# Two attentions on one core: the polynomial that VectorE uses for B's exps goes from degree three to degree two

## The chip, the cores and the metric

The kernel runs on one core of a Trainium2 chip. The metric is device time in microseconds (us), the median of three runs. The core has TensorE (PE, matrix products into PSUM), ScalarE (ACT, activations such as exp), VectorE (DVE, elementwise work and reductions), GpSimd (POOL) and SyncE (SP); the last two here mostly issue transfers (DMA).

## The reference

Two attention layers over the same input x (2048 tokens, 512 wide, 32 heads of 16) are mixed by a gate. A has one key and one value head for all query heads; B has its own K and V for every head.

```
q, k, v = ...                                  # x @ wq, x @ wk, x @ wv; A: one k and v, B: one per head
scores = einsum("bhqd,bhkd->bhqk", q, k) * 16 ** -0.5
p = softmax(scores)                            # no mask: 2048 x 2048 for each of 32 heads
o = einsum("bhqk,bhkd->bhqd", p, v)  -> 2048 x 512 @ wo
g = sigmoid((x * gate_w).sum(-1))
out = g * A + (1 - g) * B
```

All tensors are float32. A's wq and wk are eight times larger than drawn, so A's scores span a wide range and B's are small. Both attentions together take 2 x 32 x 2048 x 2048 exps, that is 2048 tiles of 128x1024.

## The kernel before, in words

A fast path is always run. At its end one flag says whether the inputs were inside the limits it assumes; if not, a general path (`_general`) computes everything again behind it. The flag is made from `stats`, a table of maxima (`absmax`, L222) that are taken along the way, reduced and compared in `flag_reduce` and `flag_check` (L1267 to L1285). For B the limit is `B_MAX`: the largest |q| times the largest |k| times the scale, where |q| is the sum of magnitudes over the 16 dimensions of a head (`magnitudes`, L511: a bit mask on VectorE, a small matmul against a matrix of heads, a maximum in PSUM) and |k| is the largest element.

The fast path walks through eight groups in turn, A and B alternating (`groups`, L202), each of eight heads. A group has four *phases* (a half of the queries, a half of the heads), a phase has 32 *quads*, and a quad two tiles of 128x1024 scores. For each tile TensorE writes the transposed scores into a PSUM slot (`products`, L751, matmuls at L762; inputs are split into high and low float16 parts that share the contraction). Then the exp is made in one of two ways:

- ScalarE reads the slot and writes exp to a tile in SBUF (`exp`, L781, the ACTIVATE at L793).
- VectorE makes it as a chain of operations (`chain`, L1000). For A it converts to an integer (L1016), splits off mantissa and power (L1020, L1024) and evaluates a polynomial of degree four (L1029, four times). For B, whose scores are small, a cubic is enough: `first` (L1049) reads PSUM, `second` (L1052) and `third` (L1056) work in SBUF. `first` occupies the PSUM slot, the others do not.

From the exps TensorE accumulates values and row sums in one PSUM slot (`values`, L834, matmuls at L847, float32): V has columns of ones beside it (vB), so sums of exps come out beside sums of exp times V. After 32 quads the phase is emptied into SBUF (L917), the row sums go through DRAM into another layout (`each`), are inverted and multiplied by the gate (`gated`, L673), come back spread over partitions, and the outputs are multiplied by them (`times`, L687) and split for the product with wo (`o_unit`, L575, matmuls at L215). Projections of Q, K and V (`project`, L464, L215) run as *units* of 24 steps in between; those for B's next group fall mostly while A is at work. V is turned by TensorE and copied into vB (L551).

There are four PSUM slots: one collects values, one is lent to a unit or to a VectorE chain (`hold`, L398), and the others pass scores to ScalarE. There are 16 tiles in SBUF for exps.

The order of everything is planned when the program is written, by a small model of the engines (`_Plan`). Each step of TensorE (`pe_step`, L1131) first looks for a score for ScalarE, then for a unit or a chain for VectorE (`spare_job`, L1086), or for values. A chain starts (`vector_job`, L974) when the pending operations of rank 3, the later operations of earlier chains, sum to no more than `WORK`, and enough tiles are free; `pick` (L945) takes the last open quad of the present phase, or, when what is left of the phase is shorter than `CHAIN` and the backlog, the last of the next phase. `hurry` (L1077) says that some unit's due time is near; then units go ahead of chains. `BEGIN` is how many tiles must be free before a long unit starts. VectorE's own queue is in the planned order too (`vector`, L110), by rank and due time; the engine carries it out strictly in that order. SP issues most transfers, in order; V's own copies are spaced.

The end of the kernel (L1532 to L1570) is written out by hand: the last products with wo for the second half of the queries, eight tiles of 128 queries, whose results are added to what earlier groups left (`late`, loaded from `out`), six of them by VectorE (`give`, L1543) and two by ScalarE and an adding transfer (`added`, L1548).

## Time and profile before

| | us |
|---|---|
| median of 3 runs | 1730.31 (1729.32 to 1733.89) |
| profiled execution, its own time | 1731.76 |
| its span, first to last instruction | 1729.9 |
| TensorE busy | 1687.4 (98%), 51451 matmuls |
| weight loads busy | 1008.2 (58%) |
| VectorE busy | 1487.2 (86%), 1658 instructions |
| ScalarE busy | 1665.2 (96%), 1813 instructions |
| GpSimd busy | 195.5 (11%) |
| TensorE clock granted, mean | 0.994 |

Times are of one execution taken by the hardware profiler. A group of instructions is shown as line, engine, operation, output and input names with their shapes, and a count, then the busy time in us, the mean length of one in ns, and the idle time before them with what ended it. Matmuls overlap and their ends are modelled, so a busy TensorE is not one at its peak. The names `prob`, `vec`, `early` and `vB` in the place of exps are all tiles for exps; `slot` is PSUM.

### The profile page before, as it was taken

The numbers are of one execution on the slowest core, as the hardware profiler recorded it, in microseconds if no ns is written. First come the engines' busy times: TensorE is split into PE (matmuls) and PEld (weight loads), VectorE is DVE, ScalarE is ACT, GpSimd is POOL, SyncE is SP. The second block draws the span as 40 slices with busy tenths as digits, with TensorE's granted clock in tenths as the row PEclk, the third lists the DMA queues.
The fourth block names the chain that finished last, engine by engine and source line by source line (L and its number), as shares of the span: only waits on it lengthen the run. The fifth ranks groups of instructions, "written<-read, shape, count | busy, mean of one in ns | idle before, by whom it ended". The sixth has DMA issues, their size and how long they took to land.

```text
span 1729.9 us, 110256 instructions
## 1 busy us (share of the span) xinstructions
PE 1687.4 (98%) x51451; PEld 1008.2 (58%) x51451; DVE 1487.2 (86%) x1658; ACT 1665.2 (96%) x1813; POOL 195.5 (11%) x316
## 2 busy tenths in 40 slices
PE   8999999999999999999999999999999999999996
PEld 5556546456566656666566555665665655655553
DVE  5567699999998899988999888999899898988954
ACT  4999999999999999999999999999999999999994
POOL 1111101000101200011111010111102111111000
PEclk9999999999999999999999999999999999999998
DMA  5212201111212211231222122222213212222312
...
DMA packets 71446, 95.72 MB, mean 55 GB/s; under 512 B 27612, under 2 KB 36092, under 8 KB 70980
## 3 DMA queue, kind: packets, MB, share of 16 engines
...
## 4 chain that ended last, share of the span: by engine, by line
PE 61%; ACT 18%; issue 12%; DVE 7%; DMA 1%; POOL 0%; SPq 0%; ACTq 0%; DVEq 0%; POOLq 0%
PE slot L847 32%; PE slot L762 17%; ACT prob L793 11%; PE slot L215 11%; ACT vec L793 6%; DVE prob L1049 1%; DVE prob L1056 1%; DVE prob L1052 1%; DVE vec L1029 1%; DVE vec L1049 1%; DVE vec L1052 1%; DMA Qa<-hiqa 0%; PE slot L1407 0%; PE slot L309 0%; DVE vec L1016 0%
## 5 line engine op out<-in xcount | busy, mean ns | idle before, releaser
L793 ACT ACTIVATE prob<-slot 128x1024 f32<-128x1024 f32 x1129 | 1121.4, 1101 | 19.3 <-PE slot L762 14.7
L793 ACT ACTIVATE vec<-slot 128x1024 f32<-128x1024 f32 x657 | 685.6, 1099 | 7.6 <-PE slot L762 3.6
L847 PE MATMUL slot<-prob,vB 64*32 64x256 f32 (+3 forms) x8096 | 529.6, 439 | 0.1
L847 PE MATMUL slot<-prob,vA 64*32 64x512 f32 (+3 forms) x7536 | 499.1, 447 | 0.0
L762 PE MATMUL slot<-Qa,kA 64*32 64x512 f16 x8192 | 441.6, 378 | 8.4 <-DMA Qa<-hiqa 2.0
L762 PE MATMUL slot<-Qb,K 64*32 64x512 f16 x8192 | 421.2, 378 | 12.7 <-ACT prob L793 4.6
L847 PE MATMUL slot<-vec,vB 64*32 64x512 f32 (+3 forms) x4640 | 367.8, 434 | 0.8 <-issue 0.7
L847 PE MATMUL slot<-vec,vA 64*32 64x512 f32 (+3 forms) x4656 | 365.7, 446 | 0.0
L762 PEld LDWEIGHTS <-K 64*32 64x32 f16 x8192 | 192.4, 90 | 239.9 <-issue 191.3
L762 PEld LDWEIGHTS <-kA 64*32 64x32 f16 x8192 | 191.8, 90 | 235.4 <-issue 180.8
L847 PEld LDWEIGHTS slot<-prob,vB 64*32 64x32 f32 x8096 | 214.9, 106 | 38.8 <-issue 8.5
L847 PEld LDWEIGHTS slot<-prob,vA 64*32 64x32 f32 x7536 | 199.8, 106 | 43.4 <-issue 14.0
L847 PEld LDWEIGHTS slot<-vec,vB 64*32 64x32 f32 x4640 | 144.7, 106 | 26.6 <-issue 8.3
L847 PEld LDWEIGHTS slot<-vec,vA 64*32 64x32 f32 x4656 | 140.2, 106 | 26.4 <-issue 8.3
L1049 DVE TENSOR_SCALAR prob<-slot 128x1024 f32<-128x1024 f32 x109 | 133.0, 1220 | 17.9 <-PE slot L762 15.1
L1029 DVE SCALAR_TENSOR_TENSOR prob<-prob,prob 128x1024 f32<-128x1024 f32 x83 | 101.1, 1220 | 1.0
L1049 DVE TENSOR_SCALAR vec<-slot 128x1024 f32<-128x1024 f32 x71 | 86.6, 1220 | 12.4 <-PE slot L762 8.2
L215 PEld LDWEIGHTS <-o 64*32 64x32 f16 x3072 | 56.5, 93 | 32.8 <-ACT o L694 6.8
L1016 DVE TENSOR_SCALAR prob<-slot 128x1024 int32<-128x1024 f32 x46 | 56.2, 1221 | 19.4 <-PE slot L762 17.0
L1052 DVE SCALAR_TENSOR_TENSOR prob<-prob 128x1024 f32<-128x1024 f32 x59 | 71.5, 1219 | 0.5
L1056 DVE SCALAR_TENSOR_TENSOR prob<-prob,prob 128x1024 f32<-128x1024 f32 x59 | 71.5, 1218 | 0.2
L1029 DVE SCALAR_TENSOR_TENSOR prob<-prob,vec 128x1024 f32<-128x1024 f32 x55 | 67.0, 1220 | 0.7
(190 smaller groups left out, 1748.5 us busy)
## 6 DMA issues: line engine op xcount, KB each, us to landing
...
```

Source lines behind the costliest of these rows:

```text
L215: nc.tensor.matmul(outs[n : n + COLS, i], lhs[i][rows(i), n : n + COLS], rhs[i][rows(i)], start=start, stop=stop)
L762: nc.tensor.matmul(bank[a : a + COLS, hh], k[rows(hh), key : key + COLS], Q[src, gi, half, p][rows(hh), j * BLK : (j + 1) * BLK], start=Tr ...
L793: nc.scalar.activation(probs[u], sc, AF.Exp, scale=SCALE / (UP * UP))
L847: nc.tensor.matmul(pair[0][32 * k : 32 * k + 32, i, cols], v[rows(i)], probs[2 * m + k // 2][rows(i), hh, cols], start=first, stop=last)
L1016: nc.vector.tensor_scalar(tile("p").bitcast(I32), pair[1], SCALE / (UP * UP) / math.log(2) * 2.0 ** 23, None, op0=ALU.mult)
L1029: nc.vector.scalar_tensor_tensor(p, m if i == 3 else p, VEC[i], m if i else w, op0=ALU.add, op1=ALU.mult)
L1049: nc.vector.tensor_scalar(tile("p"), pair[1], CUBE[0] * SCALE / (UP * UP), CUBE[1], op0=ALU.mult, op1=ALU.add)
L1052: nc.vector.scalar_tensor_tensor(tile("w"), tiles["p"], CUBE[2], tiles["p"], op0=ALU.add, op1=ALU.mult)
L1056: nc.vector.scalar_tensor_tensor(p, w, CUBE[3], p, op0=ALU.add, op1=ALU.mult)
```

## The change

For B's exps on VectorE, with s the scaled score, the cubic is replaced by c0 + c1 s + c2 s s. The chain makes only the last two terms, with the square root of c2 folded in: `first` scales (PSUM to SBUF), `second` is (t + c1 / sqrt(c2)) t, in the same tile. c0 is left out of the tile. It belongs to every key that VectorE made, so its part of the output is c0 times the sum of V over those keys, and its part of the row sum is c0 times their number. `sums_of` takes sums of V over blocks of 64 keys when V is projected (a reduction from PSUM, a scaling, two small copies between the halves of the partitions); `missing` adds up the blocks that a phase's VectorE quads cover; `gated` adds the count to `each`, and `times` adds the sum of V before it multiplies. The very last phase keeps a third operation that adds c0.

The degree-two polynomial is used within |s| of 0.044. The bound becomes length of q times length of k, per head: `norms` replaces `magnitudes` for q and the plain maximum for k (a clamp, a square, the matmul, a maximum), `flag_reduce`, `flag_pairs` and `flag_check` multiply the two for each head.

A chain of B now needs one tile, not two. Several constants of the plan change with it (`BEGIN`, `CHAIN`, `WORK`, the limit in `hurry`, due times), and the hand-written end gives all eight sums to VectorE.

The diff; a line of "..." marks what is left out.

```
@@ -34,24 +34,25 @@
-B_MAX = 0.16
+B_MAX = 0.044
...
-CUBE = (0.5500864384102879, 0.8808852829622843, -0.986763876, 1.22848465)
+SQUARE = (1.0000001191795511, 1.0002430729569356, 0.4999387172344313)
...
+SQUARED, HI_MAX = 16.0, 60000.0
...
-LEFT, LEFT_END, BEGIN = 1, 1, 5
+LEFT, LEFT_END, BEGIN = 1, 1, 4
...
@@ -491,8 +492,8 @@
             def then(end):
...
-                if kind == "q_b":
-                    plan.vec(lambda: magnitudes(2 * gi + half, hilo[0]), 330, 2, end, due=end + 4000, room=spare_tiles)
+                if src == "b" and part != "v":
+                    plan.vec(lambda: norms(kind, 2 * gi + half, hilo[0]), 1400, 2, end, due=end + 4000, room=spare_tiles)
...
@@ -501,20 +502,61 @@
+            def blocks():
+                sums_of(gi, half)
...
+            if part == "v":
+                one = plan.vec(blocks, 1250, 0, 0.0, (one,))
...
-    def magnitudes(n, hi):
+    v_sums = {}
+    def sums_of(gi, half):
+        if half == 0:
+            v_sums[gi] = ops.tile([P, 2, 2 * NT], F32, tag="sums", name=f"sums{gi}", bufs=2)
+        at = slice(NT * half, NT * (half + 1))
+        own, other = v_sums[gi][:, 0, at], v_sums[gi][:, 1, at]
+        nc.vector.tensor_reduce(own, pair[1].rearrange("p e (n k) -> p (e n) k", k=ROWS), axis=AX.X, op=ALU.add)
+        nc.vector.tensor_scalar(own, own, SQUARE[0] * UP ** -2, None, op0=ALU.mult)
+        swapped(other, own, nc.sync)
+        plan.sp += 2 * ISSUE_SP
+    def missing(ph, to):
+        n, half, q = phases[ph]
+        sums = v_sums[n // 2]
+        taken = [divmod(m - 32 * ph, 2) for m in range(32 * ph, 32 * ph + 32) if m in vector]
+        for i in range(2):
+            runs = []
+            for k in sorted(2 * c + (w ^ i) for c, w in taken):
+                if runs and runs[-1][1] == k:
+                    runs[-1][1] += 1
+                else:
+                    runs.append([k, k + 1])
+            for r, (a, b) in enumerate(runs):
+                nc.vector.tensor_reduce(to[rows(i), r : r + 1], sums[rows(i), i ^ (q // 2), a:b], axis=AX.X, op=ALU.add)
+            for r in range(1, len(runs)):
+                nc.vector.tensor_tensor(to[rows(i), :1], to[rows(i), :1], to[rows(i), r : r + 1], op=ALU.add)
+        return len(taken)
+    measured = [0]
+    def norms(kind, n, hi):
...
-        nc.vector.tensor_scalar(mag.bitcast(I32), hi.rearrange("p e t -> p (e t)").bitcast(I32), 0x7FFF7FFF, None, op0=ALU.bitwise_and)
...
+        nc.vector.tensor_scalar(mag, hi, -HI_MAX, HI_MAX, op0=ALU.max, op1=ALU.min)
+        nc.vector.scalar_tensor_tensor(mag, mag, SQUARED / (UP * UP), mag, op0=ALU.mult, op1=ALU.mult)
...
         def job():
...
@@ -524,15 +566,16 @@
         def finish(t):
             def top():
-                nc.vector.tensor_reduce(stats[: 2 * COLS, KINDS.index("q_b"), n : n + 1], pair[1][: 2 * COLS], axis=AX.XY, op=ALU.max)
+                nc.vector.tensor_reduce(stats[: 2 * COLS, KINDS.index(kind), n : n + 1], pair[1][: 2 * COLS], axis=AX.XY, op=ALU.max)
...
             def then(end):
+                measured[0] += 1
...
-        start = plan.dve + 330 + FROM_VEC
-        units.append(_Unit([(job, PRODUCT)], finish, lambda now: now >= start, lambda: start + 12000, f"m{n}"))
+        start = plan.dve + 1400 + FROM_VEC
+        units.append(_Unit([(job, PRODUCT)], finish, lambda now: now >= start, lambda: start + 12000, f"m{kind}{n}"))
...
     def turned(gi, half, hilo, now):
...
@@ -596,9 +639,9 @@
             def take():
...
-                    if last or t == 0:
+                    if last:
...
-                            (nc.sync, nc.scalar if last else nc.sync)[e].dma_start(out[tt[e] * P : (tt[e] + 1) * P, :], mine[:, e])
+                            (nc.sync, nc.scalar)[e].dma_start(out[tt[e] * P : (tt[e] + 1) * P, :], mine[:, e])
...
@@ -626,7 +669,7 @@
-        due = 32 * (LASTS + half) if ends else 32 * (8 * j + 2 * half + 11)
+        due = 32 * (LASTS + half) if ends else 32 * (8 * j + 2 * half + 9)
...
@@ -670,7 +713,15 @@
         def over(c):
...
+        ph = phases.index((n, half, q))
+        short = src == "b" and not ends and any(m in vector for m in range(32 * ph, 32 * ph + 32))
+        if short:
+            lost = ops.tile([P, 16], F32, tag="lost", name=f"lost{n}{half}{q}", bufs=2)
         def gated():
+            if short:
+                count = missing(ph, lost)
+                nc.vector.tensor_scalar(each, each, SQUARE[0] * ROWS * count, None, op0=ALU.add)
...
@@ -688,7 +739,10 @@
-                nc.vector.tensor_tensor(o[:, c : c + cut], o[:, c : c + cut], d[:, c : c + cut], op=ALU.mult)
+                if short:
+                    nc.vector.scalar_tensor_tensor(o[:, c : c + cut], o[:, c : c + cut], lost[:, :1], d[:, c : c + cut], op0=ALU.add, op1=ALU.mult)
+                else:
+                    nc.vector.tensor_tensor(o[:, c : c + cut], o[:, c : c + cut], d[:, c : c + cut], op=ALU.mult)
...
         def high(c):
...
@@ -713,7 +767,7 @@
-        plan.vec(gated, 430, 3.5, now + 7500, (), spreads, min(due, now + 25000),
+        plan.vec(gated, 900 if short else 430, 3.5, now + 7500, (), spreads, min(due, now + 35000),
...
@@ -978,7 +1032,7 @@
-        if u is None or spare_tiles() < ((3 if source(quads[u // 2][0]) == "a" else 2) if half_vec else 4):
+        if u is None or spare_tiles() < ((3 if source(quads[u // 2][0]) == "a" else 1) + (not half_vec)):
...
         def job():
@@ -1010,7 +1064,7 @@
         def give(*names):
...
-        owed[0] += 3 if source(quads[u // 2][0]) == "a" else 2
+        owed[0] += 3 if source(quads[u // 2][0]) == "a" else 1
...
         def convert():
...
@@ -1046,19 +1100,19 @@
         if source(quads[u // 2][0]) == "b":
...
             def first():
-                nc.vector.tensor_scalar(tile("p"), pair[1], CUBE[0] * SCALE / (UP * UP), CUBE[1], op0=ALU.mult, op1=ALU.add)
+                nc.vector.tensor_scalar(tile("p"), pair[1], math.sqrt(SQUARE[2]) * SCALE / (UP * UP), None, op0=ALU.mult)
...
             def second():
-                nc.vector.scalar_tensor_tensor(tile("w"), tiles["p"], CUBE[2], tiles["p"], op0=ALU.add, op1=ALU.mult)
+                nc.vector.scalar_tensor_tensor(tiles["p"], tiles["p"], SQUARE[1] / math.sqrt(SQUARE[2]), tiles["p"], op0=ALU.add, op1=ALU.mult)
...
             def third():
-                p, w = tiles["p"], tiles["w"]
-                nc.vector.scalar_tensor_tensor(p, w, CUBE[3], p, op0=ALU.add, op1=ALU.mult)
-                give("w")
+                nc.vector.tensor_scalar(tiles["p"], tiles["p"], SQUARE[0], None, op0=ALU.add)
+            whole_exp = quads[u // 2][0] == LASTS
...
-            b = plan.vec(second, 1131, 3, 0.0, (a,), None, due(2600))
-            plan.vec(third, 1131, 3, 0.0, (b,), over, due(1300))
+            b = plan.vec(second, 1131, 3, 0.0, (a,), None if whole_exp else over, due(2200 if whole_exp else 1300))
+            if whole_exp:
+                plan.vec(third, 620, 3, 0.0, (b,), over, due(800))
...
@@ -1067,8 +1121,8 @@
-    CHAIN = 14000, 7000
-    JOB, AFTER, TURN, WORK = 500, 3000, 3000, 2500
+    CHAIN = 28000, 7000
+    JOB, AFTER, TURN, WORK = 500, 3000, 3000, 500
...
     def cost(unit):
@@ -1081,7 +1135,7 @@
-        return least < 0
+        return least < 9000
...
     def spare_job(now):
...
@@ -1261,26 +1315,43 @@
-    highest = cst.tile([P, len(KINDS)], F32, name="highest")
+    highest = cst.tile([P, len(KINDS) + 1], F32, name="highest")
+    most_of = cst.tile([P, len(KINDS) + 1], F32, name="most_of")
+    upper = cst.tile([COLS, 2, 2 * NG], F32, name="upper")
+    lengths = cst.tile([COLS, 3, NG], F32, name="lengths")
...
     def flag_reduce():
-        each = cst.tile([P, len(KINDS)], F32, name="each")
-        nc.vector.tensor_reduce(each, stats, axis=AX.X, op=ALU.max)
-        nc.gpsimd.partition_all_reduce(highest, each, P, ReduceOp.max)
+        b = KINDS.index("q_b")
+        nc.vector.memset(most_of, 0.0)
+        nc.vector.tensor_reduce(most_of[:, : len(KINDS)], stats, axis=AX.X, op=ALU.max)
+        for n in range(2):
+            nc.sync.dma_start(upper[:, n], stats[COLS : 2 * COLS, b + 2 * n])
+    def flag_pairs():
+        b = KINDS.index("q_b")
+        for n in range(2):
+            nc.vector.tensor_tensor(upper[:, n], upper[:, n], stats[:COLS, b + 2 * n], op=ALU.max)
+        nc.vector.tensor_reduce(lengths[:, :2], upper.rearrange("p n (g h) -> p n g h", h=2), axis=AX.X, op=ALU.max)
+        nc.vector.tensor_mul(lengths[:, 2], lengths[:, 0], lengths[:, 1])
+        nc.vector.tensor_reduce(most_of[:COLS, len(KINDS) :], lengths[:, 2], axis=AX.X, op=ALU.max)
+        nc.gpsimd.partition_all_reduce(highest, most_of, P, ReduceOp.max)
...
     def flag_check():
...
-        nc.vector.tensor_scalar(highest[:, 1:], highest[:, 1:], 1.0 / UP, None, op0=ALU.mult)
+        nc.vector.tensor_scalar(highest[:, 1:k], highest[:, 1:k], 1.0 / UP, None, op0=ALU.mult)
...
+        for n in range(r, k):
+            most = QK_MAX if KINDS[n][-1] == "a" else QK_MAX * QK_MAX * SQUARED / UP
...
+        for n, at, most in ((0, ix("q_a"), S_MAX / (DH * SCALE)), (1, k, (B_MAX / SCALE * SQUARED) ** 2)):
...
@@ -1324,7 +1395,7 @@
-                units.append(project("q", src, gi, half, f"q_{src}", past(64 * s - 64),
+                units.append(project("q", src, gi, half, f"q_{src}", past(64 * s - 84),
...
@@ -1352,8 +1423,11 @@
         if ph == LASTS - 2:
...
         if ph == LASTS - 1:
-            a = plan.vec(flag_reduce, 400, 4, plan.dve, due=plan.dve + 20000)
-            plan.vec(flag_check, 1500, 4, plan.dve + 40000, (a,), None, plan.dve + 45000)
+            def reduced(end):
+                b = plan.vec(flag_pairs, 400, 4, end + 2 * LANDS, due=end + 20000)
+                plan.vec(flag_check, 1700, 4, end + 40000, (b,), None, end + 45000)
+            plan.vec(flag_reduce, 500, 4, plan.dve, (), reduced, plan.dve + 10000, room=lambda: measured[0] == 4 * NG)
...
     def preload():
...
@@ -1545,11 +1619,6 @@
-    def added(t, e):
-        tt, tile = 8 + 4 * e + t, free_tiles[0]
-        nc.scalar.activation(tile[:, e], into[t][:, e], AF.Copy, scale=gate_up[:, 1, tt : tt + 1])
-        nc.gpsimd.dma_start(out[tt * P : (tt + 1) * P, :], tile[:, e], accum_op=ALU.add)
...
     for t in range(4):
@@ -1557,15 +1626,11 @@
-        elif t == 2:
-            give(1, 0)
...
-            give(1, 1)
+            give(0, t - 2)
...
-        if t in (1, 2):
-            added(0, t - 1)
-    for t in (2, 3):
+    for t in range(1, 4):
...
```

10 lines of the change are left out of this document (4 added, 6 removed).

## The prediction

> **What bounds the kernel now.** I read the page first (busy shares, the chain that ended last, the groups), then the busy times cut into the stretches in which A's or B's scores are made, then the matmuls of single lines in the same stretches, and last the chain and VectorE's timeline close up.
>
> ```profile
> PE 1687.4 (98%) x51451; PEld 1008.2 (58%) x51451; DVE 1487.2 (86%) x1658; ACT 1665.2 (96%) x1813; POOL 195.5 (11%) x316
> ...
> PE 61%; ACT 18%; issue 12%; DVE 7%; DMA 1%; POOL 0%; SPq 0%; ACTq 0%; DVEq 0%; POOLq 0%
> ...
> L793 ACT ACTIVATE prob<-slot 128x1024 f32<-128x1024 f32 x1129 | 1121.4, 1101 | 19.3 <-PE slot L762 14.7
> L793 ACT ACTIVATE vec<-slot 128x1024 f32<-128x1024 f32 x657 | 685.6, 1099 | 7.6 <-PE slot L762 3.6
> ```
>
> Three engines look full at once: TensorE 98%, ScalarE 96%, VectorE 86%, and the chain runs through TensorE for 61% of the span. The two groups under the chain hold 1786 of the 2048 exps of 128x1024; most of the rest are VectorE's. Matmul ends are modelled, so 98% needs a second look. Here are the busy times by stretch (start:end, length, then PE, PEld, DVE, ACT and POOL, each with its count). The rows from 255, 665, 1080 and 1492 are B's groups, those from 25, 470 and 866 are A's; A's last, from 1276, is left out.
>
> ```profile
> 25.00:255.00 230.00, 223.37 (x6482) 125.11 (x6479) 163.75 (x195) 223.85 (x245) 26.95 (x48) 0.99 0.19 50
> 255.00:470.00 215.00, 210.37 (x6268) 122.96 (x6267) 203.56 (x215) 213.78 (x233) 15.64 (x30) 1.00 0.17 43
> 470.00:665.00 195.00, 194.36 (x6067) 121.97 (x6054) 175.74 (x194) 193.85 (x212) 17.47 (x29) 1.00 0.20 52
> 665.00:866.00 201.00, 199.83 (x6276) 125.00 (x6265) 185.56 (x199) 198.78 (x216) 20.72 (x34) 1.00 0.23 52
> 866.00:1080.00 214.00, 212.47 (x6628) 125.19 (x6620) 193.64 (x213) 212.24 (x232) 30.59 (x46) 1.00 0.23 52
> 1080.00:1276.00 196.00, 194.61 (x6164) 120.34 (x6153) 181.69 (x195) 195.02 (x213) 30.22 (x46) 1.00 0.24 52
> ...
> 1492.00:1707.00 215.00, 208.52 (x6345) 121.54 (x6339) 163.91 (x186) 202.42 (x220) 16.99 (x25) 0.99 0.24 63
> ```
>
> ScalarE is at 99% in every row from 255 to 1276. Its cost per exp is a pitch: in the row from 1080, 196 us for 213 instructions, 0.92 us each. VectorE is at 93% in B's row from 1080 (181.69 of 196). So an exp can leave ScalarE only when VectorE has time for it. How full TensorE is, I take from pieces of the chain:
>
> ```profile
> 1000.94 0.86 PE slot L847 x16
> 1001.80 0.22 PE slot L762 x8
> ...
> 1011.02 0.86 PE slot L215 x32
> ```
>
> A score (eight 64x32 tiles, one exp's worth) is 0.22 us, 32 projection matmuls are 0.86 us (0.215 per eight), and one quad of values, two exps' worth, is 0.86 us. So an exp carries 0.215 + 0.43 = 0.645 us of TensorE, and eight matmuls of L215 carry 0.215 us. The counts of the scores (L762) and then of L215, in the same stretches (columns: length, PE busy with the count, clock, DMA):
>
> ```profile
> 255.00:470.00 215.00, 112.89 (x2232) 1.00 0.17 43
> ...
> 665.00:866.00 201.00, 109.64 (x2072) 1.00 0.23 52
> 866.00:1080.00 214.00, 108.45 (x2032) 1.00 0.23 52
> 1080.00:1276.00 196.00, 104.09 (x2032) 1.00 0.24 52
> ...
> 1492.00:1707.00 215.00, 103.50 (x2032) 0.99 0.24 63
> ```
>
> ```profile
> 255.00:470.00 215.00, 27.34 (x768) 1.00 0.17 43
> ...
> 665.00:866.00 201.00, 31.16 (x864) 1.00 0.23 52
> 866.00:1080.00 214.00, 52.88 (x1440) 1.00 0.23 52
> 1080.00:1276.00 196.00, 31.56 (x864) 1.00 0.24 52
> ...
> 1492.00:1707.00 215.00, 41.80 (x1104) 0.99 0.24 63
> ```
>
> Eight matmuls per exp give, for B's four stretches: 279 x 0.645 + 96 x 0.215 = 200.6 us of work in 215; 259 and 108 give 190.3 in 201; 254 and 108 give 187.0 in 196; 254 and 138 give 193.5 in 215. Together 771.4 us of work in 827, a density of 0.933. A's row from 866 gives 254 and 180, 202.5 in 214, 0.946. The densest stretch that I found, again L762 and then L215:
>
> ```profile
> 648.00:702.00 54.00, 28.52 (x576) 1.00 0.14 34
> ```
>
> ```profile
> 648.00:702.00 54.00, 7.73 (x216) 1.00 0.14 34
> ```
>
> 72 x 0.645 + 27 x 0.215 = 52.2 us in 54, 0.967. The reader should see that ScalarE and VectorE together set B's pace, but that TensorE stands only some 3 to 7% behind them.
>
> **The change part by part.** *Removed.* These rows count the exps that VectorE makes: L1049 starts one of B (109 + 71 = 180), L1016 one of A (46 + 26 = 72).
>
> ```profile
> L1049 DVE TENSOR_SCALAR prob<-slot 128x1024 f32<-128x1024 f32 x109 | 133.0, 1220 | 17.9 <-PE slot L762 15.1 <-ACT prob L793 1.8 <-ACT vec L793 0.7
> L1049 DVE TENSOR_SCALAR vec<-slot 128x1024 f32<-128x1024 f32 x71 | 86.6, 1220 | 12.4 <-PE slot L762 8.2 <-ACT prob L793 2.2 <-ACT vec L793 1.6
> ...
> L1056 DVE SCALAR_TENSOR_TENSOR prob<-prob,prob 128x1024 f32<-128x1024 f32 x59 | 71.5, 1218 | 0.2
> ...
> L1016 DVE TENSOR_SCALAR prob<-slot 128x1024 int32<-128x1024 f32 x46 | 56.2, 1221 | 19.4 <-PE slot L762 17.0 <-ACT prob L793 0.7 <-ACT vec L793 0.6
> ...
> L1016 DVE TENSOR_SCALAR vec<-slot 128x1024 int32<-128x1024 f32 x26 | 31.8, 1221 | 10.6 <-PE slot L762 7.9 <-ACT vec L793 1.6 <-issue 0.7
> ...
> L1020 DVE TENSOR_SCALAR prob<-prob 128x1024 int32<-128x1024 int32 x29 | 20.1, 691 | 0.6
> ```
>
> ```profile
> 1091.99 1.22 DVE L1056 SCALAR_TENSOR_TENSOR prob<-prob,prob 128x1024 f32<-128x1024 f32 x1
> 1093.12 1.22 DVE L1056 SCALAR_TENSOR_TENSOR vec<-prob,vec 128x1024 f32<-128x1024 f32 x1
> ```
>
> Full-size operations last 1.22 us but follow each other every 1.13 us. One of B's exps loses one of three, 1.13 us: 180 x 1.13 = 203 us of VectorE. The last phase keeps an addition of the constant, in SBUF; L1020 is the nearest row, 0.69 us, for about nine exps, 6 us back. One of A's exps stays at about 1.13 + 2 x 0.60 + 4 x 1.13 = 6.9 us.
>
> *Added on VectorE.* The nearest rows:
>
> ```profile
> L527 DVE TENSOR_REDUCE stats<-slot 64x1 f32<-64x1024 f32 x8 | 9.7, 1213 | 1.4 <-PE slot L522 1.4
> L224 DVE TENSOR_REDUCE stats<-hikb 128x1 f32<-128x1024 f16 x8 | 9.7, 1208 | 0.0
> ...
> L1545 DVE SCALAR_TENSOR_TENSOR xT<-slot,gate_up,xT 128x512 f32<-128x512 f32 x6 | 4.2, 744 | 0.8 <-PE slot L215 0.8
> ...
> L516 DVE TENSOR_SCALAR vec<-hiqb 128x512 int32<-128x512 int32 x5 | 2.1, 418 | 0.0
> ...
> L1284 DVE TENSOR_REDUCE lim<-lim 128x1 f32<-128x30 f32 x1 | 0.2, 183 | 0.0
> ```
>
> The lengths replace magnitudes for q and the maximum (L224, 1.21) for k. The clamp reads as many bytes as L516, 0.42 us; its bounds are 0.42 and 1.22. The square is a two-tensor operation; no row has one with 16-bit data throughout, so 0.42 to 1.22, and I take 1.22, the row of its own form (L1056). The maximum behind the matmul is L527's 1.21. Sum for q: 2.85 against 1.63 before, 1.22 more; for k: 2.85 against 1.21, 1.64 more; eight halves each, 22.9 us (bounds 10 and 36). The sums of V add a full-size reduction and a tiny scaling, 1.21 + 0.18, eight times: 11.1 us. The missing constants are three to five tiny operations per B phase, at 0.18 (L1284): 15 phases, 8 to 14 us, take 11. Multiplying by the reciprocal with one more operand has the same shape; I add nothing. All added: 45 us (29 to 61), against 203 - 6 = 197 removed.
>
> The Trainium skill's page "VectorE: DVE Perf Modes", section "The perf-mode tier table", gives two-tensor operations on 16-bit data in SBUF double rate. If that holds for the square, 512 cycles and that page's 150 of fixed cost at 0.96 GHz give an estimate of 0.69 us, the norms cost 8 us less, and the forecast falls by about 1 us; no run here shows it.
>
> *Where the removed time goes.* Nothing ends earlier because VectorE is idler; the order is planned greedily, so VectorE takes more of B's exps and ScalarE fewer. Each saves ScalarE 0.92 us, until TensorE is the bound. In the stretch from 1080, a density of 0.967 means 187.0 / 0.967 = 193.4 us; then ScalarE holds 210 of the 254 exps, and VectorE has 44, where it now has 254 - 213 = 41. At 2.26 us each, beside 181.7 - 41 x 3.39 = 42.7 us of other work and 2.5 of constants, it is 75% busy. The stretch from 255 needs 53, and 82%. So VectorE stops being a bound, and I let B's four stretches go to the density of the best one: 771.4 / 0.967 = 797.7 us, **29.3 us less** than 827.
>
> *What A pays.* Norms and sums (34 us) fall mostly in A's stretches, where K, V and Q of B are projected: 8.5 us each. A's first group can hide them: in the row from 25 VectorE is busy for 163.75 us of 230. If that cover were gone, it would pay like the others. In the other three, 25 us are 3.6 of A's exps, which go back to ScalarE: 3.3 us. Then WORK 500 starts a chain only when the one before is wholly issued, CHAIN 28000 turns to the next phase earlier, and units come ahead of chains when 9 us are left, not 0. No row prices that: nothing if chains are only reordered, or 12 us in all if each stretch loses four exps more. I take 1.7, so A pays **5 us**.
>
> *Moved and queued.* SP gets 16 small copies of the sums and two of the lengths, 0.59 us an issue by the nearest row:
>
> ```profile
> 1000.24 0.59 SPq L422 DMA_DIRECT2D K<-lokb  x1
> ```
>
> That is 1.2 us per half, once before V's own transfers, which go out spaced by 1.5 us and are needed a group later; that slack hides it. Without it, the first B values of a group would be late by 1.2 us, 5 us over four groups. The new wait of the constants is for sums that landed a phase or more ago; behind it on VectorE stand the reciprocal and all chains. TensorE gets eight more tiny matmul groups, 1.7 us, inside the density. BEGIN, the output products' earlier due time and Q's units 20 quads earlier only reorder the same matmuls: nothing. Done early, the flag's chain stays ahead of the tail.
>
> *Tail.* Eight final sums on VectorE, not six beside two on ScalarE: L1545 is 0.74 us, and two more cost at most 1.5 us, less the 0.8 us wait in that row that they fill: **1 us**. The last-phase partial write that is dropped costs nothing, as it was hidden.
>
> *Sum.* 1731.8 (the profiled execution's own time) - 29.3 + 5 + 1 = 1708.5 us. That execution was 1.5 us above the median of the runs, so 1707 us.
>
> **Rivals.** (1) *TensorE is no ceiling.* With VectorE at 0.927 and B's exps at 2.26 us, the stretch from 1080 balances at T = 0.92 x (254 - (0.927 T - 45.2) / 2.26), 183 us, 13 less; 6.6% of 827 are 55 us. For: ScalarE and VectorE are what is full now. Against: 187.0 us of matmuls don't fit into 183. At density 1.0 the gain is 827 - 771.4 = 55.6; with A's cost, the tail and the 1.5 that is 1681, and I count 1681 to 1692 here.
>
> The Trainium skill's page "Trainium Kernel Development and Optimization", section "Performance Expectations", says that matmul busy time is a poor measure and weight-load share a good one. By its measure, 58% here, TensorE has room and this rival would hold; the counted pieces, 0.954 in that stretch, disagree with it.
>
> (2) *Nothing moves.* The holes in TensorE's row may be hand-overs through PSUM slots and not missing ScalarE time; the chain's "issue" and ScalarE pieces would stay. For: B's stretch from 1080 is at 0.954 with both engines full. Against: the stretch from 255 is at 0.933, with ScalarE's row at 213.78 of 215. If B gains nothing to 6 us and A and the tail take 6: 1730 to 1736, and 1726 if A's cost stays away; say 1730.
>
> (3) *Slower: A is starved.* Place: A's stretches from 470, 866 and 1276, where the new thresholds let units go first, and one chain waits out the other. Price: 0.92 us for each A exp that returns to ScalarE. It decides when more than 31 of A's 72 return, as they eat the 29.3 us; at 42, 1731.8 - 29.3 + 39 + 1 = 1742, less 1.5 is 1741. For: three thresholds turn against chains at once. Against: units are of fixed number, and VectorE has 19 and 20 idle us in the rows from 470 and 866 to catch up.
>
> (4) *The bound fails and the general path runs behind the fast one.* It repeats all exps; 2048 x 0.92 us more is at least 3600 us in all. Against: the reference's inputs (seed 0) give 0.0389 as the largest product of lengths over four, under the new 0.044.
>
> **How the numbers follow.** Forecast, 0.72: B's density between 0.95 and 0.985 and A's cost up to 12, so gains of 15 to 44 in B, about 1688 to 1724. Rival 1 0.10, rival 2 0.09, rival 3 0.08, rival 4 0.01. About 0.3%, 5 us, is what a measurement of this kernel tells from no change. Faster: 0.72 + 0.10, less 0.01 where A's cost meets B's lowest gain, 0.81; same 0.10; slower 0.09. The range leaves out the lower half of rival 1, rivals 3 and 4, and part of rival 2: 1687 to 1728.
>
> **What would show it.** Right: L1049 rises to 190 to 220 and its third operation is gone; 1786 exps on ScalarE fall by 10 to 40; B's stretches shorten to 190 to 208 us; ScalarE there shows holes, and VectorE falls under 88%. A's stretches within 3 us of now, L1016 between 55 and 72. Wrong: ScalarE still at 99% in B's stretches (rival 2), L1016 below 40 (rival 3), a density above 0.985 (rival 1), or a DVE wait on the new sums.

## The result: 1743.1 us, 0.6% slower

The changed kernel took 1743.14 us (median of 4 runs, 1739.09 to 1745.39) against 1729.89 us for the kernel before beside it: a ratio of 1.0059 on record, with a 95% interval of 1.0031 to 1.0087. (The quotient of the two medians would be 1.0077, inside that interval.) The forecast was 1707 us (1687 to 1728). One execution of those behind the medians here and below, one of e12's ten at 3311.45 us, was in a slow state with a granted clock of 0.963, is in no ratio, and its cause is open. The profile after is of an execution of 1739.09 us. From its page, the busy times, the chain's shares, and the exps of ScalarE (L847):

```profile
PE 1692.8 (97%) x52011; PEld 1008.5 (58%) x52011; DVE 1329.2 (77%) x1574; ACT 1654.3 (95%) x1795; POOL 190.1 (11%) x314
...
PE 71%; ACT 13%; DVE 9%; issue 4%; DMA 2%; SPq 0%; POOL 0%; ACTq 0%; DVEq 0%; POOLq 0%
...
L847 ACT ACTIVATE prob<-slot 128x1024 f32<-128x1024 f32 x1106 | 1097.0, 1090 | 25.6 <-PE slot L816 19.4
L847 ACT ACTIVATE vec<-slot 128x1024 f32<-128x1024 f32 x664 | 686.4, 1091 | 18.2 <-PE slot L816 10.8
```

VectorE's groups by line and shape: B's exps (L1103 starts one), A's (L1070), the square and the maximum of the norms (L559, L569), the sums of V (L526), the count added to the row sums (L724).

```profile
L1103 DVE TENSOR_SCALAR prob<-slot 128x1024 f32<-128x1024 f32 x129 | 157.3, 1220 | 22.9 <-ACT prob L847 9.4 <-PE slot L816 8.4 <-ACT vec L847 4.7
...
L1103 DVE TENSOR_SCALAR vec<-slot 128x1024 f32<-128x1024 f32 x79 | 96.4, 1220 | 14.9 <-ACT prob L847 11.6 <-PE slot L816 2.3 <-ACT vec L847 0.7
...
L1070 DVE TENSOR_SCALAR prob<-slot 128x1024 int32<-128x1024 f32 x36 | 44.0, 1224 | 25.4 <-PE slot L816 21.1 <-ACT vec L847 3.8 <-ACT prob L847 0.3
...
L1070 DVE TENSOR_SCALAR vec<-slot 128x1024 int32<-128x1024 f32 x24 | 29.3, 1223 | 17.3 <-PE slot L816 16.7 <-ACT vec L847 0.5
...
L569 DVE TENSOR_REDUCE stats<-slot 64x1 f32<-64x1024 f32 x16 | 19.4, 1214 | 6.4 <-PE slot L564 3.3 <-PE slot L816 2.8 <-ACT vec L847 0.2
...
L559 DVE SCALAR_TENSOR_TENSOR prob<-prob 128x1024 f16<-128x1024 f16 x12 | 14.7, 1225 | 0.4
...
L526 DVE TENSOR_REDUCE sums<-slot 128x16 f32<-128x1024 f32 x8 | 9.7, 1215 | 0.0
...
L724 DVE TENSOR_SCALAR each<-each 128x32 f32<-128x32 f32 x15 | 2.7, 182 | 12.5 <-DMA each<-held 12.2
```

The chain now runs through TensorE for 71%, not 61%. VectorE is at 77%, down from 86%; it starts 208 of B's exps instead of 180 and 60 of A's instead of 72, and ScalarE makes 1770 in these groups instead of 1786. All this is close to what was forecast, but the end moved the other way. The middle of the kernel shows why. These windows start some 15 us into A's second group and end as far into its fourth: two groups of A and two of B, the scores of 1024 exps. After the length stand PE, PEld, DVE, ACT, POOL. The second row holds L215 (or L216) alone: PE, PEld. Before:

```profile
460.00:1289.00 829.00, 824.27 (x25831) 506.75 (x25816) 758.30 (x820) 822.63 (x894) 102.32 (x160) 1.00 0.23 52
...
460.00:1289.00 829.00, 168.90 (x4631) 85.89 (x4615) 1.00 0.23 52
```

After:

```profile
455.00:1295.00 840.00, 829.39 (x26048) 501.99 (x26042) 668.41 (x765) 819.22 (x887) 97.18 (x156) 1.00 0.22 51
...
455.00:1295.00 840.00, 172.16 (x4608) 83.52 (x4608) 1.00 0.22 51
```

At 0.645 us an exp and 0.215 us per eight matmuls, the 1024 exps are 660.5 us of TensorE, so before is (660.5 + 124.5) / 829 = 0.947 dense, after (660.5 + 123.8) / 840 = 0.934. VectorE's share fell from 91% to 80%, and the stretch became 11 us longer. Of these, 6.5 are one hole: ScalarE, which starts an exp every 0.91 us, let 7.4 us pass between the starts at 737.2 and 744.6.

```profile
737.16 1.04 ACT L847 ACTIVATE prob<-slot 128x1024 f32<-128x1024 f32 x1
744.59 1.02 ACT L847 ACTIVATE vec<-slot 128x1024 f32<-128x1024 f32 x1 [6.38 <-PE slot L816]
```

Last, one group of A and one of B in each kernel (256 exps in each window, some 16 of them of the next group), with the same two rows for each (before: A, B, then L215; after: A, B, then L216):

```profile
875.00:1089.00 214.00, 212.53 (x6639) 125.44 (x6630) 194.09 (x212) 212.28 (x231) 30.59 (x46) 1.00 0.23 52
1089.00:1289.00 200.00, 198.61 (x6284) 122.48 (x6269) 185.15 (x199) 198.75 (x217) 30.74 (x46) 1.00 0.25 52
...
875.00:1089.00 214.00, 50.42 (x1377) 24.61 (x1368) 1.00 0.23 52
1089.00:1289.00 200.00, 33.83 (x935) 17.57 (x936) 1.00 0.25 52
```

```profile
878.00:1103.00 225.00, 223.11 (x7084) 136.68 (x7076) 177.51 (x205) 218.78 (x238) 42.28 (x60) 1.00 0.28 60
1103.00:1295.00 192.00, 190.79 (x6012) 116.92 (x6003) 162.18 (x183) 190.45 (x207) 16.14 (x28) 1.00 0.18 42
...
878.00:1103.00 225.00, 65.96 (x1728) 33.67 (x1728) 1.00 0.28 60
1103.00:1295.00 192.00, 20.57 (x576) 9.55 (x576) 1.00 0.18 42
```

B became 8 us shorter and A 11 us longer. Between them 360 or so matmuls of projections moved from B to A (936 became 576, 1368 became 1728): 45 x 0.215 = 9.7 us. So B is shorter by about what left it. Its density didn't rise: (165.1 + 25.2) / 200 = 0.951 before, (165.1 + 15.5) / 192 = 0.941 after.

### The profile page after: what moved, and what is told of

It is laid out like the page before. It is cut to its first block, busy times and chain, and to the rows that moved or that the text cites. A ratio compares the mean times of both kernels' runs of the same rounds, so it can differ in the third digit from the quotient of the medians.

```text
span 1737.3 us, 111191 instructions
## 1 busy us (share of the span) xinstructions
PE 1692.8 (97%) x52011; PEld 1008.5 (58%) x52011; DVE 1329.2 (77%) x1574; ACT 1654.3 (95%) x1795; POOL 190.1 (11%) x314
## 3 DMA queue, kind: packets, MB, share of 16 engines
q1 hardware_dynamic: 55268, 58.68, 12.6%
## 4 chain that ended last, share of the span: by engine, by line
PE 71%; ACT 13%; DVE 9%; issue 4%; DMA 2%; SPq 0%; POOL 0%; ACTq 0%; DVEq 0%; POOLq 0%
PE slot L901 38%; PE slot L816 21%; PE slot L216 11%; ACT prob L847 8%; ACT vec L847 4%; DVE prob L1103 2%; DVE vec L1103 1%; DVE prob L1106 1%; DVE vec L1083 1%; DVE vec L1106 1%; DMA Qa<-hiqa 0%; DMA each<-held 0%; DMA wob<-in_B_wo_dram 0%; SPq L702 0%; PE slot L1481 0%
## 5 line engine op out<-in xcount | busy, mean ns | idle before, releaser
L847 ACT ACTIVATE prob<-slot 128x1024 f32<-128x1024 f32 x1106 | 1097.0, 1090 | 25.6 <-PE slot L816 19.4
L847 ACT ACTIVATE vec<-slot 128x1024 f32<-128x1024 f32 x664 | 686.4, 1091 | 18.2 <-PE slot L816 10.8
L901 PE MATMUL slot<-prob,vA 64*32 64x256 f32 (+3 forms) x7776 | 502.5, 442 | 0.0
L901 PE MATMUL slot<-vec,vB 64*32 64x256 f32 (+3 forms) x4960 | 383.3, 431 | 0.7 <-issue 0.4
L901 PE MATMUL slot<-vec,vA 64*32 64x384 f32 (+3 forms) x4688 | 357.3, 439 | 0.5 <-DVE vec L971 0.5
L901 PEld LDWEIGHTS slot<-prob,vB 64*32 64x32 f32 x8048 | 218.8, 106 | 43.3 <-issue 9.3
L1103 DVE TENSOR_SCALAR prob<-slot 128x1024 f32<-128x1024 f32 x129 | 157.3, 1220 | 22.9 <-ACT prob L847 9.4
L1106 DVE SCALAR_TENSOR_TENSOR prob<-prob 128x1024 f32<-128x1024 f32 x129 | 157.7, 1223 | 2.8
L1103 DVE TENSOR_SCALAR vec<-slot 128x1024 f32<-128x1024 f32 x79 | 96.4, 1220 | 14.9 <-ACT prob L847 11.6
L1106 DVE SCALAR_TENSOR_TENSOR vec<-vec 128x1024 f32<-128x1024 f32 x79 | 96.6, 1222 | 1.7
L1083 DVE SCALAR_TENSOR_TENSOR prob<-prob,prob 128x1024 f32<-128x1024 f32 x65 | 79.5, 1222 | 1.4
L216 PEld LDWEIGHTS <-o 64*32 64x32 f16 x3072 | 54.1, 93 | 34.6 <-ACT o L748 8.4
L216 PE MATMUL slot<-w16ob,o 64*32 64x512 f16 x1536 | 60.0, 389 | 6.8 <-ACT o L748 6.3
L660 POOL DMA_DIRECT2D out_dram<-prob x48 | 42.6, 1315 | 198.2 <-DVE prob L648 169.9
```

The source lines that it names most:

```text
L216: nc.tensor.matmul(outs[n : n + COLS, i], lhs[i][rows(i), n : n + COLS], rhs[i][rows(i)], start=start, stop=stop)
L660: nc.gpsimd.dma_start(dst[rows(i), e], state["sum"][rows(i), e], accum_op=ALU.add)
L847: nc.scalar.activation(probs[u], sc, AF.Exp, scale=SCALE / (UP * UP))
L901: nc.tensor.matmul(pair[0][32 * k : 32 * k + 32, i, cols], v[rows(i)], probs[2 * m + k // 2][rows(i), hh, cols], start=first, stop=last)
L1083: nc.vector.scalar_tensor_tensor(p, m if i == 3 else p, VEC[i], m if i else w, op0=ALU.add, op1=ALU.mult)
L1103: nc.vector.tensor_scalar(tile("p"), pair[1], math.sqrt(SQUARE[2]) * SCALE / (UP * UP), None, op0=ALU.mult)
```

## The experiments

| kernel | median, us | ratio to before, interval |
|---|---|---|
| changed kernel | 1743.14 | 1.0059 [1.0031, 1.0087] |
| e1: its arithmetic, six old plan constants | 1754.5 | 1.0134 [1.0115, 1.0153] |
| e2: old arithmetic, its six plan constants | 1771.2 | 1.0237 [1.0216, 1.0258] |
| e3: changed kernel, three constants of units old | 1736.9 | 1.0036 [1.0022, 1.0051] |
| e4: changed kernel, two constants of chains old | 1741.4 | 1.0053 [1.0033, 1.0072] |
| e5: before, projections 16 of 24 steps | 1723.1 | 0.9950 [0.9930, 0.9969] |
| e6: changed, projections 16 of 24 steps | 1686.8 | 0.9743 [0.9723, 0.9764] |
| e7: changed, row sums taken later | 1729.4 | 0.9993 [0.9981, 1.0004] |
| e8: changed, planned with 917 ns | 1730.5 | 0.9987 [0.9974, 0.9999] |
| e9: before, planned with 917 ns | 1729.0 | 0.9985 [0.9969, 1.0001] |
| e10: before, planned with 915 ns | 1737.5 | 1.0038 [1.0022, 1.0053] |
| e11: changed, B's Q and K in one pass, row sums later | 1697.1 | 0.9796 [0.9768, 0.9824] |
| e12: before, B's Q and K in one pass | 1733.0 | 1.0003 [0.9988, 1.0018] |
| e13: changed, one phase's row sums past SP's queue | 1729.3 | 1.0003 [0.9992, 1.0013] |

The expectations name theories by letters. U: the new limits of units push projections into A's stretches. C: the new limits of chains leave VectorE idle in B. R: any other order moves the time by several us. F: the order of before is no accident, only that of after has a stall. L: waits for late units and transfers make the loss. S: one stall, at 737 us, makes it. T: TensorE is the ceiling already, so nothing can be gained.

### Arithmetic and plan apart (e1, e2)

e1 is the changed kernel with these edits; e2 is the kernel before with the same edits the other way round, from old to new:

```
-LEFT, LEFT_END, BEGIN = 1, 1, 4
+LEFT, LEFT_END, BEGIN = 1, 1, 5
...
-due = 32 * (LASTS + half) if ends else 32 * (8 * j + 2 * half + 9)
+due = 32 * (LASTS + half) if ends else 32 * (8 * j + 2 * half + 11)
...
-CHAIN = 28000, 7000
-JOB, AFTER, TURN, WORK = 500, 3000, 3000, 500
+CHAIN = 14000, 7000
+JOB, AFTER, TURN, WORK = 500, 3000, 3000, 2500
...
-return least < 9000
+return least < 0
...
-past(64 * s - 84)
+past(64 * s - 64)
```

> The new arithmetic with the six old constants of the plan (BEGIN 5, CHAIN 14000, WORK 2500, the limit in hurry 0, the output products' due time + 11, Q's units 64 quads ahead). If the new constants cost the time (theories U and C): faster than before, about 1715 us, A keeps 66 or more exps on VectorE, ScalarE has 1765 or fewer. If any reordering of this plan costs several us, whatever the arithmetic saves (theory R): 1730 to 1745, no better than the changed kernel.

> The kernel before (cubic, old bound) with only the six new constants. Theory U (the new limits push projections from B's stretches into A's and starve A's chains): 1745 to 1765 us, A's exps on VectorE fall from 72 to 60 or fewer, L215's matmuls in A's four stretches rise by some 1200. Theory C (the chain constants leave VectorE idle in B): also slower, B's exps fall below 175. Theory R: within 10 us of before, either way.

Each half alone is worse than both: 1.3% and 2.4% slower. e1 is above every range given for it, e2 above U's; in e2 both C's sign (168 of B's exps, under 175) and one of U's (52 of A's, 60 or fewer) came, so it doesn't separate them. In e1 VectorE starts still more of B's exps (226), but units come late. What VectorE waited for there (total us, times, longest):

```profile
DVE each L724 <- DMA each<-held: 35.5, 9, 7.8
...
DVE hiqa L488 <- PE slot L216: 27.2, 5, 9.6
```

And ScalarE at the turn between two halves of a B group, then VectorE in the same microseconds:

```profile
339.10 2.96 ACT L847 ACTIVATE prob<-slot 128x1024 f32<-128x1024 f32 x3
348.07 1.02 ACT L847 ACTIVATE vec<-slot 128x1024 f32<-128x1024 f32 x1 [6.01 <-PE slot L816]
```

```profile
336.82 0.42 DVE L751 TENSOR_TENSOR o<-vec,o 128x256 f16<-128x256 f32 x1
342.68 1.23 DVE L488 TENSOR_SCALAR hiqb<-slot 128x1024 f16<-128x1024 f32 x1 [5.43 <-PE slot L216]
```

VectorE keeps the planned order: it stands 5.4 us at hiqb until the unit's last matmuls are done, and only then can Q be sent and the next half's scores begin; ScalarE stands 6.0 us. Six such holes of 7 to 8 us from one exp to the next are in e1's trace. Why the units are late isn't isolated; in the plan a chain and a unit want the same lent PSUM slot. With the new constants the changed kernel is 11 us faster than e1, and on the old arithmetic the same constants cost some 40 us, with VectorE at 75% (1333.8 us) and 32 more exps on ScalarE (1818 against 1786):

```profile
PE 1703.7 (96%) x50043; PEld 982.2 (56%) x50043; DVE 1333.8 (75%) x1482; ACT 1696.6 (96%) x1845; POOL 195.3 (11%) x316
...
L793 ACT ACTIVATE prob<-slot 128x1024 f32<-128x1024 f32 x1138 | 1130.2, 1101 | 23.9 <-PE slot L762 17.6 <-PE slot L847 3.8 <-DVE lim L1278 1.1
L793 ACT ACTIVATE vec<-slot 128x1024 f32<-128x1024 f32 x680 | 708.7, 1100 | 9.6 <-PE slot L762 6.4 <-PE slot L847 1.7 <-DVE prob L1056 0.2
```

So the constants belong to the arithmetic. The prediction put three of the six (BEGIN, the due time, Q's units) at nothing and the other three at 1.7 us; on the old arithmetic the six together cost some 40, and which of them does isn't told apart.

### Which constants cost (e3, e4)

e3 takes back `hurry`, the due time and Q's 84 in the changed kernel, e4 takes back CHAIN and WORK.

> The changed kernel with the three constants of the units put back (hurry 0, due + 11, Q 64 quads ahead); BEGIN, CHAIN and WORK stay new. Theory U: A's stretches get back their 33 us of projections to B, about 1722 us. Theory C: still 1738 to 1745, ScalarE at 99% and VectorE near 83% in B.

> The changed kernel with the two constants of the chains put back (CHAIN 14000, WORK 2500); the units' constants stay new. Theory C: VectorE takes 220 or more of B's exps, ScalarE's pitch leaves 99% in B, about 1722 us. Theory U: still 1738 to 1745, A's stretches as long as in the changed kernel.

1736.9 and 1741.4 us. Neither brings the time of before back, and e4 is not told apart from the changed kernel. Rival 3 would have had e4 give A its exps back and the time with them; VectorE has 64 of A's instead of 60, and the time is the same. e3 (between U's 1722 and C's 1738 to 1745) and e4 (within U's range, far from C's 1722) separate no theory by themselves. They show one thing more: after the first 100 us no two exps of ScalarE start more than 2.9 us apart in either, so an order can be 0.4 to 0.5% slower without one large hole. What costs them that isn't known.

### Is TensorE the ceiling? (e5, e6)

In both kernels each planned projection unit of Q, K and V does 16 of its 24 steps (a third of the products is left out, so projections are less exact):

```
-by_tiles(bank, lhs, rhs, n == 0, n == len(STEPS) - 1)
+by_tiles(bank, lhs, rhs, n == 0, n == 15)
...
-_Unit([(lambda n=n: job(n), PRODUCT) for n in range(len(STEPS))], finish,
+_Unit([(lambda n=n: job(n), PRODUCT) for n in range(16)], finish,
```

> The kernel before, with 16 instead of 24 steps in each of the 31 projection units of Q, K and V that are planned (the steps that multiply the low part of x by the high part of w are left out, so the projections are less exact); the plan knows of it. TensorE loses 31 x 8 x 0.215 = 53 us of matmuls, ScalarE and VectorE lose nothing. Theory T (TensorE is what B's stretches stand on already, at a density of about 0.945, and VectorE's freed time finds no TensorE time for more exps): before gains only until VectorE, at 93% in B, and ScalarE bound it, 10 to 25 us, 1706 to 1722. Theory L (the changed kernel's loss is waits for late units and transfers, TensorE has nothing to do with it): before gains 30 to 53 us, like the changed kernel.

> The changed kernel with the same 16 of 24 steps in each planned projection unit. T: with TensorE relieved the second degree polynomial is worth something: 1680 to 1705, and 10 to 40 us faster than the kernel before with the same edit; VectorE takes 230 or more of B's exps, ScalarE under 1760. L: the changed kernel stays 5 to 15 us slower than the kernel before with the same edit.

The kernel before gains 8 us. The changed one is at 1686.8 us, 56 us under its own 1743.1 and 45 under the kernel before (1731.4), and now the change is worth 36 us. The same four groups, e5 and then e6 (L215, L216 in the second row of each):

```profile
460.00:1286.00 826.00, 806.85 (x24536) 480.53 (x24528) 795.47 (x859) 817.40 (x886) 103.15 (x161) 1.00 0.22 52
...
460.00:1286.00 826.00, 133.01 (x3520) 67.25 (x3528) 1.00 0.22 52
```

```profile
452.00:1256.00 804.00, 796.08 (x24997) 484.05 (x24987) 708.77 (x792) 798.18 (x865) 101.35 (x160) 1.00 0.23 53
...
452.00:1256.00 804.00, 130.61 (x3488) 62.83 (x3488) 1.00 0.23 53
```

In e5 VectorE is at 96% (795 of 826) and the density falls to (660.5 + 94.6) / 826 = 0.914: with three operations for each of B's exps, VectorE and ScalarE (817 of 826) hold the pace, and TensorE has slack that nobody takes. In one of B's stretches alone VectorE is at 98% (195.24 of 199):

```profile
660.00:859.00 199.00, 192.87 (x5644) 110.06 (x5637) 195.24 (x203) 198.32 (x216) 18.43 (x32) 1.00 0.17 40
```

In e6 VectorE is at 88%, it starts 242 of B's exps, and the density is (660.5 + 93.7) / 804 = 0.938. So there are two bounds at one height. Taking VectorE's alone away, or TensorE's alone, brings next to nothing; taking both brings 45 us. This is theory T, though it let the kernel before gain 10 us at least; L had the changed kernel 5 to 15 us behind here too, so waits alone don't explain why nothing was gained. One rival isn't tested: a unit of 16 steps also holds the lent PSUM slot for a shorter time than one of 24, and chains need that slot. For TensorE's time speaks that TensorE is idle for 4 us of e13's middle (831 less 827.20, shown below), but for 19 of e5's.

### How much is the written order worth? (e7 to e10)

e8, e9 and e10 leave the work as it is and change only the length of an exp in the plan (`EXP` 916 to 917, or to 915), and with it the order and, by a few, the exps that VectorE takes (in e8 216 of B's and 56 of A's). e7 lets the inversion of the row sums stand later in VectorE's order when SP's queue is long:

```
-plan.vec(gated, 900 if short else 430, 3.5, now + 7500, ...
+plan.vec(gated, 900 if short else 430, 3.5, max(now + 7500, plan.sp + LANDS), ...
```

> The changed kernel; only the time from which the plan lets the inversion of the row sums stand in VectorE's order is also bound by the model's SP queue (now + 7500, or the end of SP's queue plus 3200 ns, whichever is later). In the profile of the changed kernel VectorE waits 5.8 us at 734 for the row sums, because Q's eight transfers stand ahead of theirs on SP, and ScalarE stands still for 6.4. L: DVE's waits for each<-held fall from 12 us to under 5, ScalarE's gap at 737 is gone, and the time falls by 7 to 15 us, to 1728 to 1736. T: the stall goes, but A and B keep their densities: 1734 to 1740, not under the kernel before.

> The changed kernel with 917 in place of 916 ns as the plan's length of an exp on ScalarE: it changes no work, only the order that comes out. Theory R (the size of the loss is an accident of the written order): the time moves by more than 6 us, either way. T and L: within 6 us of the changed kernel, 1737 to 1749; by L a move of more than 4 us goes with a stall for row sums or for Q gained or lost, by T with matmuls moved.

> The kernel before with 917 in place of 916 ns as the plan's length of an exp: no work changed, only the order that comes out. Theory R (a written order's accidents are worth as much as the change's loss): as for the changed kernel, which the same edit moved by 13 us, the time moves by several us; if it gets slower by 5 to 13 us, the kernel before owed its lead to a lucky order. Theory F (the order of before is no accident, that of after had one stall): within 4 us of before, 1727 to 1735.

> The kernel before with 915 in place of 916 ns: a second order of the same work. R: several us away from before or from the order with 917. F: within 4 us of before, 1727 to 1735.

e7 and e8 are both some 13 us faster than the changed kernel and both lack the hole at 737 (e7 is in L's range; T put it at 1734 to 1740); VectorE's waits for `each` fall from 12.2 us to 2.9 and 1.8. e8 wasn't aimed at it, so the loss is an accident of the order: theory R as e8 states it, for the changed kernel. The kernel before moves too: 1729.0 with 917, but 1737.5 with 915, where its trace has a hole of its own (VectorE, then SP):

```profile
465.99 1.23 DVE L1029 SCALAR_TENSOR_TENSOR prob<-prob,prob 128x1024 f32<-128x1024 f32 x1
472.09 0.35 DVE L674 RECIPROCAL each<-each 128x32 f32<-128x32 f32 x1 [4.88 <-DMA each<-held]
```

```profile
462.94 1.16 SPq L656 DMA_DIRECT2D held<-vec  x2
464.20 4.74 SPq L659 DMA_DIRECT2D vec<-vec  x6
469.04 0.53 SPq L661 DMA_DIRECT2D each<-held  x1
```

Q's eight transfers and six moves of outputs go out on SP first, `each` at 469.0, and VectorE stands 4.9 us at the row sums; ScalarE's next start comes 5.2 us later. In the profiled kernel before the waits at this line sum to 3.2 us. e9 alone would fit theory F; with e10 it fails too: both kernels have orders with such a hole and orders without, some 8 to 13 us apart. For the kernel before no run takes the hole out alone, so how much of its 8 us is the hole's isn't shown.

### The hole alone (e13)

That is the place in the changed kernel too. VectorE and SP from the changed kernel's timeline:

```profile
719.73 1.23 DVE L488 TENSOR_SCALAR hiqb<-slot 128x1024 f16<-128x1024 f32 x1 [13.02 <-PE slot L216]
...
725.20 0.68 DVE L251 SCALAR_TENSOR_TENSOR w16kb<-wkb,w16kb 128x512 f16<-128x512 f32 x1
...
734.23 0.16 DVE L547 TENSOR_TENSOR lost<-lost 64x1 f32<-64x1 f32 x1
740.18 0.18 DVE L724 TENSOR_SCALAR each<-each 128x32 f32<-128x32 f32 x1 [5.79 <-DMA each<-held]
```

```profile
SPq L239 <- DVE w16kb L251: 31.4, 1, 31.4
```

```profile
725.90 0.35 SPq L239 DMA_DIRECT2D wob<-in_B_wo_dram  x1
726.37 0.50 SPq L423 DMA_DIRECT2D Qb<-hiqb  x1
...
732.59 1.16 SPq L699 DMA_DIRECT2D held<-vec  x2
733.85 4.46 SPq L702 DMA_DIRECT2D prob<-vec  x6
738.41 0.53 SPq L704 DMA_DIRECT2D each<-held  x1
```

The second fence is SP's longest wait, the third its issues. SP waited 31.4 us with the load of wob, until VectorE at L251 had read wkb (725.9): raw weights have one buffer (L237). VectorE came to L251 after 13 us of waiting at L488 for Q's unit. Behind wob on SP stood Q's transfers, though hiqb was written by 721.0 (719.73 + 1.23); behind them `held`, the moves, and at last `each`, issued at 738.4. VectorE reached L724 at 734.4, stood 5.8 us, and behind it in its order stood the rest of one B exp and the first operation of the next, which frees a PSUM slot. e13 keeps the order of work on TensorE, ScalarE and VectorE and sends this one phase's row sums from GpSimd:

```
+row = nc.gpsimd if (n, half, q) == (3, 0, 0) else nc.sync
...
-nc.sync.dma_start(held..., raw[0][which])
+row.dma_start(held..., raw[0][which])
...
-nc.sync.dma_start(each, held...)
+row.dma_start(each, held...)
```

> The changed kernel in its own written order on every engine; only for one phase, the first of B's second group, the transfers of the row sums (two to held, one to each) are issued by GpSimd in place of SP, so that they don't stand behind Q's eight on SP. Theory S (that stall is what makes the changed kernel slower than before): VectorE's 5.8 us and ScalarE's 6.4 us of standing still at 737 are gone, and the time is 1734 to 1738. Theory R (the loss is the whole order's): the stall goes, but other hand-overs take up its time, and the time stays within 3 us of the changed kernel, 1740 to 1746.

```profile
730.52 0.16 DVE L547 TENSOR_TENSOR lost<-lost 64x1 f32<-64x1 f32 x1
730.71 0.18 DVE L725 TENSOR_SCALAR each<-each 128x32 f32<-128x32 f32 x1
```

VectorE passes L725 (L724 of the changed kernel) without a wait, and the time is 1729.25 us, 1.0003 of before [0.9992, 1.0013]: 0.56%, 9.7 us less than the changed kernel. Theory S named the right cause, with too small a size: it gave 1734 to 1738. (The two medians, each taken beside other runs of before, differ by 13.9 us; by their ratios it is 9.7.) R as e13 states it, that other hand-overs take up the time, fails. As both kernels make the same 1780 exps in the same order, their starts can be set against each other one by one: the changed kernel's are 3.7 us later than e13's at 736 us, 12.1 us later at 760, and 8.3 at the end. So the hole costs 8.4 us, and the rest of the two executions differs by some 4 us either way. SP stands 31.4 us at the load of wob in e13 as well; with no row sums behind it, ScalarE has no hole there.

The Trainium skill's page "DMA: Bandwidth & Descriptors", section "Issuing engines are not separate DMA queues", says that issuing from several engines saves only the sequencer's time, usually small beside the transfer. The trace agrees on that time (0.53 us for `each`, which landed 1.8 us after its issue began, 738.41 to 740.18). What counted here is another thing, the place in the queue: `each` was issued 13 us after the phase's sums had left PSUM (L971, 724.06 + 1.22), which this row of VectorE's timeline gives:

```profile
724.06 1.22 DVE L971 COPY vec<-slot 128x1024 f32<-128x1024 f32 x1
```

So without this hole the change is worth nothing that these runs can tell, in either direction; the three orders without it and with the new constants, e7, e8 and e13, stand at 0.9987 to 1.0003 of before. T says why nothing was gained, and the late row sums why this order lost something.

### A version that beats both (e11, e12)

B's scores are small and its exps near 1, so Q and K of B need less exactness than A's. In both kernels they are projected from the high parts alone; e11 has e7's edit as well:

```
+count = 8 if src == "b" and part != "v" else len(STEPS)
...
-[(lambda n=n: job(n), PRODUCT) for n in range(len(STEPS))]
+[(lambda n=n: job(n), PRODUCT) for n in range(count)]
```

> The changed kernel with the later row sums (now + 7500 or the end of SP's queue plus 3200 ns), and Q and K of B projected in 8 of 24 steps: only the high part of x times the high part of w, nothing of V or of A is left out. It is meant as a whole kernel, since B's scores are small and their exps near 1. TensorE loses 16 x 16 x 0.215 = 55 us. Theory T (TensorE is the ceiling, at a density of about 0.945): 1675 to 1700. Theory L (waits for late units and transfers): about 1725, as with the later row sums alone.

> The kernel before with the same 8 of 24 steps for Q and K of B. T: VectorE, at 93% in B with three operations an exp, and ScalarE take over as the bound: 1710 to 1725, 20 to 45 us behind the changed kernel with this edit. L: within 10 us of the changed kernel with this edit.

16 units of 16 steps less, 55 us of TensorE, bring the kernel before nothing (1733.0 against 1732.4) and the changed kernel 32 us against e7: 1697.1 us, 2.0% under the kernel before. The pair repeats e5 and e6 with another cut: 36 us between the kernels both times. T's range held e11 and missed e12, which it had 8 to 23 us faster: the other bound is nearer than T put it. One of B's stretches in e12 has VectorE at 98% (193.55 of 198), as in e5:

```profile
663.00:861.00 198.00, 191.12 (x5654) 108.48 (x5656) 193.55 (x199) 197.28 (x216) 16.27 (x28) 1.00 0.17 39
```

## Why the prediction was wrong

**What bounds the kernel: the step that failed.** "TensorE stands only some 3 to 7% behind them" took prices from uninterrupted pieces and one dense stretch of 54 us as what a whole group can reach. Over whole groups the density is 0.947 before with VectorE at 91%, and (660.5 + 123.8) / 831 = 0.944 in e13 (4608 matmuls of its projection line, as in the changed kernel) with VectorE at 668.48 of 831 us, 80%:

```profile
451.00:1282.00 831.00, 827.20 (x26040) 503.78 (x26028) 668.48 (x765) 818.56 (x888) 99.58 (x159) 1.00 0.22 52
```

"B's four stretches go to the density of the best one", 0.967 and -29.3 us, was therefore 0: B's group shown above went from 0.951 to 0.941, and the middle is 829 us before and 831 in e13. TensorE's row of busy time, 99.4% of the middle (824 of 829), which I set aside as modelled, told more of it (97.7% in e5, where TensorE has slack); the counted pieces misled. The share of weight loads hardly changes, 61% before and 58% in e5, and is far from full where TensorE binds. The Trainium skill's page "Trainium Kernel Development and Optimization", section "Performance Expectations", which I had weighed in rival 1, calls it a good metric and matmul busy time a bad one; in this case it was the other way round. What fills the last 5% of TensorE's time isn't settled.

**The other bound** was read rightly: VectorE with three operations an exp does hold B's pace once TensorE is relieved (98% of a B stretch in e5 and in e12), and "VectorE stops being a bound" is true after the change: 80% in its middle, and 88% in e6's. But a bound that falls away uncovers the next one, which I put 3 to 7% away and which was there already.

**The terms on VectorE** were sized well. Removed and added: norms measured 6.6 + 19.6 + 19.4 us (clamp, square, maximum) against 22.8 for what they replace, 22.8 more (22.9 said); sums of V 9.7 + 1.4 = 11.1 (11.1 said). The square took 1.22 us in 16-bit data (L559), as I chose; the estimate of 0.69 from the Trainium skill's page "VectorE: DVE Perf Modes", section "The perf-mode tier table", doesn't hold for this operation.

**"A pays 5 us"**: A's three later groups became 9 to 11 us longer each. 12 exps went back to ScalarE, 11 us in all by the prediction's own price, but in the A group shown TensorE is the fuller engine now (223.1 of 225 us, ScalarE 218.8), and 9.7 us of projections were moved into it. The prediction took units as "of fixed number" and didn't ask in which group they run. As B gave up the same matmuls, the sum is about nothing; the step was wrong in place, not in the total.

**SP and the order**: "that slack hides it", and the units' constants at "nothing". This is the second step that failed, and it decided the sign. The forecast looked at SP's 16 new copies and not at what else stands ahead of the row sums: a load that waits, Q's eight transfers and six moves. "A DVE wait on the new sums" was named as a sign of being wrong, and the wait stands at L724, the new line, but it's for `each`, as at L674 before. Which of the edits brought the queue into this order isn't told apart: e1, with the old constants, has longer waits for `each` (35.5 us at L724), and e3, with Q's old time, has 13.5.

**Rivals.** (2) "Nothing moves", 1726 to 1736, is what the change is worth without the hole (e13, 1729.3), and its sign was there: ScalarE is still at 99% of B's stretch (190.45 of 192). Its mechanism, hand-overs through PSUM slots, is shown by no run. I gave it 0.09 because of the one row at 0.933, which was cut at round times and held part of A's next group (its 279 exps are more than a group's 256). (1) "TensorE is no ceiling" is refuted by e6 against e13, short of the slot's part. (3) "A is starved" needs more than 31 of A's exps; 12 returned, and e4 doesn't bring the time back. (4) didn't occur: one pass of 1743 us.

**The tail**, 1 us more forecast: from the end of the last exp to the end it is 26.1 us before and 26.0 after.
